# A convolution and a gated MLP in one kernel: how x is loaded and turned, how block 0 is convolved, and how far the second layer runs behind

## The chip, the cores and the metric

The kernel runs on one core of a Trainium2 chip. Its engines work side by side, each through its own queue in order: TensorE (PE in the profile; PEld are its weight loads), VectorE (DVE), ScalarE (ACT), GpSimd (POOL), and SyncE (SP), which here only issues DMAs and passes marks on. The metric is the device time of one execution in microseconds, the median over runs.

## The reference

x is 8 sequences of 4096 tokens with 192 columns, float32. Each of 8 heads (24 columns each) has 7 taps, passed through a softmax; the causal convolution sums a token and the six before it. Then a gated MLP with 1536 hidden columns follows:

```python
w = np.exp(weight - weight.max(-1, keepdims=True)); w = w / (w.sum(-1, keepdims=True) + 1e-9)
x_pad = np.concatenate([zeros(B, 6, D), x], axis=1)
out = np.einsum('hk,bskhg->bshg', w, windows_of_7(x_pad))     # per head h, tap k
g = out.reshape(B*S, D) @ w_gate                               # 192 -> 1536
val = out.reshape(B*S, D) @ w_val
return (g / (1 + np.exp(-g)) * val) @ w_out                    # 1536 -> 192
```

## The kernel before

**Tiles.** The 32768 tokens are 64 blocks of 512; two blocks make a pair (32 pairs). Hidden columns are 12 chunks of 128. So there are 768 chunks in all, and 24 per pair; "chunk c" below counts from the start of the run, or within a pair's 24 where it says so. The convolution works on columns in partitions and tokens along the row. A pair's 2 x 192 columns are three groups of 128 partitions: group 0 (A of the first block), group 1 (the last columns of one block with columns of the other), group 2.

**First layer.** `Block.first(j)` makes gate and val of chunk j: three matmuls of 64 rows each for gate (array rows 0 to 63) and three for val (rows 64 to 127), side by side in the array. Since a group's halves are needed on both halves of the array, each convolved group `xc` also has a copy `xs` with its halves swapped, made by two DMAs (`Group.swap`). PSUM holds 2 gate and 3 val tiles. `Block.gate(j)` lets ScalarE make silu (L318) and VectorE multiply h = silu x val (L320).

**Second layer.** `Block.second(n)` emits units. A block has 48: two halves of the tokens, in each two passes (the swap) over j = 0 to 11. Unit u of a half reads h of chunk j = u mod 12. A unit is two matmuls of 64 rows (`piece`, L325), one for each half of the array; the weights loaded are pieces of h. Here each chunk j of a block does four units of the block before: `first(j)` comes ahead of them, except where a half ends (j = 5 and 11); there the units come first, then ScalarE empties the accumulator (L363, an evacuation) and then `first(j)` follows. After the last unit of the first pass a mark is set: a no-op on SyncE that waits for it, and the first unit of the second pass waits for the mark.

**The convolution of later pairs.** `emit_cast` lets GpSimd issue a DMA that casts x to float16 in DRAM, `emit_turn` a transposing DMA from there. For each group ScalarE makes the product of tap 0 in PSUM (`start_d`, L249) and of two taps in SBUF (`act_tap`, L253), VectorE adds two taps to tap 0 (`dve_tap`, L260), GpSimd makes two products (L267), adds the parts (L273) and joins them (L277). An order written out by hand sets this: `at_chunk(c, f)` puts f behind chunk c's silu and h on every queue. For pair q the groups begin at chunk 24q-27, 24q-19 and 24q-11, their VectorE taps come 1 and 3 chunks later, ScalarE's 2 and 4, GpSimd's work 4, the swap 11.

**The opening.** x of pair 0 is loaded as it lies, cast by ScalarE and GpSimd, and turned by TensorE. The softmax is made on 8 partitions and spread by small matmuls. A0 and A1 are convolved by products as above; only group B goes through 14 matmuls with diagonal matrices (L390). Two swaps go through TensorE. The first weights come as float32 and are cast by ScalarE and GpSimd. All of this stands ahead of chunk 0, and VectorE's four taps of A1 (L260) stand ahead of its first h.

**The end.** When no first layer is left, the last block's 48 units follow, then copies and stores.

Of the kernel before, what the change touches and what calls it, by code (L numbers as in the profile page):

```python
# [12 lines left out]
PLAN = dict(  # L13
    start=(-27, -19, -11),
    first=(6, 10, 16),
    aD=0, aP=(2, 4), taps=(1, 3), pool=4, swap=11,
    cast=-54, turn=-40,
    nact=2, npool=2, gate=2, val=3,
)
# [3 lines left out]
def kernel(  # L23
# [9 lines left out]
    nc = tc.nc  # L33
# [30 lines left out]
    dpool = ctx.enter_context(tc.tile_pool(name="x16d", bufs=3, space=bass.MemoryType.DRAM))  # L64
# [3 lines left out]
    HIST = 16  # L68
    ROWS = HIST + TB
    drams, xts = {}, {}  # L70

    def emit_cast(q):
        t0 = q * 2 * TB - HIST
        d = dpool.tile([ROWS, 2 * D], fp16, tag="x16d", name="x16d")
        src = bass.AP(
            tensor=x_flat.tensor,
            offset=x_flat[t0 : t0 + 1, :].offset,
            ap=[[D, ROWS], [TB * D, 2], [1, D]],
        )
        nc.gpsimd.dma_start(out=d[:, :].rearrange("r (b c) -> r b c", b=2), in_=src)  # L80
        drams[q] = d

    def emit_turn(q):
        xt = xpool.tile([P, 3, ROWS], fp16, tag="xt", name="xt", bufs=3)
        nc.sync.dma_start(out=xt[:, :, :], in_=drams.pop(q)[:, :], transpose=True)
        xts[q] = xt

    def emit_blank(q):
        nc.scalar.copy(xts[q][:, 0, 0:HIST], zeros[:, 0:HIST])
        nc.scalar.copy(xts[q][0:DB, 1, 0:HIST], zeros[0:DB, 0:HIST])  # L90

    def sync_after(ins, earlier, why="one bank, two halves of the array"):
# [8 lines left out]
    taps = const_pool.tile([H, K], fp32, tag="taps", name="taps")  # L101
    nc.sync.dma_start(out=taps, in_=weight)
    x_sb = xpool.tile([P, 2 * SUBS, D], fp32, tag="x_sb", name="x_sb", bufs=1)
    halves = [
        nc.sync.dma_start(
            out=x_sb[:, b * SUBS : (b + 1) * SUBS, :],
            in_=x_flat[b * TB : (b + 1) * TB, :].rearrange("(s p) d -> p s d", p=P),
        )
        for b in range(2)
    ]  # L110

    C1 = 4 * P
    w = wpool.tile([P, 3, Dff], fp16, tag="w_sb", name="w_sb")
    w_st = wpool.tile([P, 3, C1], fp32, tag="w_st", name="w_st")
# [5 lines left out]
    for rows, src in w_halves:  # L120
        sync_after(
            nc.sync.dma_start(out=w_st[rows, :, :], in_=src[:, :, 0:C1]), halves[0], "x goes first"
        )

    def load_w(lo, hi, which):
        rows, src = w_halves[which]
        nc.gpsimd.dma_start(out=w[rows, :, lo:hi], in_=src[:, :, lo:hi])

    ident32 = const_pool.tile([P, P], fp32, tag="ident32", name="ident32")
    make_identity(nc, ident32)  # L130
    ident = const_pool.tile([P, P], fp16, tag="ident", name="ident")
    nc.vector.tensor_copy(ident, ident32)

    swapper = const_pool.tile([P, P], fp16, tag="swapper", name="swapper")
    nc.vector.tensor_copy(swapper[:, 0:DB], ident[:, DB:P])
    nc.vector.tensor_copy(swapper[:, DB:P], ident[:, 0:DB])
# [4 lines left out]

    opening = ctx.enter_context(ExitStack())
    pool0 = opening.enter_context(tc.tile_pool(name="xts0", bufs=1, space=bass.MemoryType.PSUM))


    zeros = const_pool.tile([P, TB], fp16, tag="zeros", name="zeros")
    nc.vector.memset(zeros, 0.0)
    early = {
        n: pool0.tile(shape, dt, tag=n, name=n)
        for n, shape, dt in (  # L150
            ("xt_act", [P, DB + TB], fp16),
            ("wn_ps", [P, 3, K], fp32),
            ("xtB", [P, DB + TB], fp16),
            ("xt", [P, DB + TB], fp16),
            ("sumB", [P, TB], fp32),
            ("swB", [P, TB], fp32),
            ("idle", [P, TB], fp32),
            ("xtC", [P, DB + TB], fp16),
        )
    }  # L160
    idle = early["idle"]

    def warm(n):
        for _ in range(n):
            nc.tensor.matmul(idle, ident, zeros, start=True, stop=True)  # L165


    own = const_pool.tile([H, 2 * D], fp32, tag="own", name="own")
    nc.gpsimd.memset(own, 1.0)
    for m in (own[:, 0:D], own[:, D:]):  # L170
        nc.gpsimd.affine_select(
            out=m, in_=m, pattern=[[1, D]],
            compare_op=ALU.is_ge, fill=0.0, base=0, channel_multiplier=-grp,
        )
        nc.gpsimd.affine_select(
            out=m, in_=m, pattern=[[-1, D]],
            compare_op=ALU.is_ge, fill=0.0, base=grp - 1, channel_multiplier=grp,
        )
    head = {n: const_pool.tile([H, 1], fp32, tag=n, name=n) for n in ("wmax", "wsum", "wrec")}
    soft = const_pool.tile([H, K], fp32, tag="soft", name="soft")  # L180
    warm(4)
    nc.vector.tensor_reduce(head["wmax"], taps, axis=AX.X, op=ALU.max, negate=True)  # L182
    nc.scalar.activation(soft, taps, AF.Exp, bias=head["wmax"])
    nc.scalar.activation(two, one, AF.Silu)
    nc.vector.tensor_reduce(head["wsum"], soft, axis=AX.X, op=ALU.add)
    nc.vector.tensor_scalar(head["wsum"], head["wsum"], scalar1=1e-9, scalar2=None, op0=ALU.add)
    nc.vector.reciprocal(head["wrec"], head["wsum"])
    nc.vector.tensor_scalar(soft, soft, scalar1=head["wrec"], scalar2=None, op0=ALU.mult)

    wn_ps = early["wn_ps"]  # L190
    wn = const_pool.tile([P, 3, K], fp32, tag="wn", name="wn")
    for g in range(3):
        nc.tensor.matmul(wn_ps[:, g, :], own[:, ts(g, P)], soft, start=True, stop=True)  # L193
    warm(2)
    nc.vector.tensor_copy(wn, wn_ps)

    x16 = xpool.tile([P, 1 + SUBS, 2, D], fp16, tag="x16", name="x16", bufs=1)
    nc.gpsimd.memset(x16[:, 0, 0, :], 0.0)
    nc.gpsimd.tensor_copy(x16[:, 1:, 0, 0:P], x_sb[:, 0:SUBS, 0:P])
    nc.scalar.copy(x16[:, 1:, 0, P:D], x_sb[:, 0:SUBS, P:D])  # L200
    nc.scalar.copy(x16[:, :, 1, 0:DB], x_sb[:, SUBS - 1 :, 0:DB])
    nc.gpsimd.tensor_copy(x16[:, :, 1, DB:D], x_sb[:, SUBS - 1 :, DB:D])
    for b in range(2):
        load_w(C1, 2 * C1, b)

# [8 lines left out]

    class Group:


        def __init__(self, p, g, pool=cpool):
            self.p, self.g, self.w, self.pool = p, g, wn[:, g, :], pool
            if p:  # L220
                self.xc_in = xts[p][:, g, HIST - pad :]
            self.parts = []

        def rows(self, s):
            return x16[:, s, :, :].rearrange("p b c -> p (b c)")[:, ts(self.g, P)]

        def turn(self, xt, reader=None):
            nc.tensor.transpose(xt[:, 0:DB], self.rows(0)[DB:P, :], ident[DB:P, DB:P])
            for s in range(SUBS):
                nc.tensor.transpose(xt[:, DB + s * P :][:, 0:P], self.rows(s + 1), ident)  # L230
            if reader == "act":
                self.xt_act = xt
            else:
                self.xt = xt

        def tap(self, k, psum=True, xt=None):
            v = (xt or self.xt)[:, DB - pad + k :][:, 0:TB] if psum else self.xc_in[:, k : k + TB]
            return v, self.w[:, k : k + 1]

        def copy(self):  # L240
            self.xc_in = self.pool.tile([P, pad + TB], fp16, tag="xcin", name="xcin")
            nc.scalar.copy(self.xc_in, self.xt[:, DB - pad :])

        def start_d(self, psum=True, xt=None):
            if self.p:
                self.aD = tpool.tile([P, TB], fp32, tag="run", name="run")
            else:
                self.aD = self.pool.tile([P, TB], fp32, tag="aD", name="aD")
            nc.scalar.mul(self.aD, *self.tap(0, psum, xt))  # L249

        def act_tap(self, k, psum=True, xt=None):
            self.parts.append(self.pool.tile([P, TB], fp32, tag=f"t{k}", name=f"t{k}"))
            nc.scalar.mul(self.parts[-1], *self.tap(k, psum, xt))  # L253

        def dve_tap(self, k, psum=False, last=False):
            v, s = self.tap(k, psum)
            run = self.aD
            if last:
                self.aD = self.pool.tile([P, TB], fp32, tag="aD", name="aD")
            nc.vector.scalar_tensor_tensor(  # L260
                out=self.aD, in0=v, scalar=s, in1=run, op0=ALU.mult, op1=ALU.add
            )

        def pool_tap(self, k):
            self.parts.append(self.pool.tile([P, TB], fp32, tag=f"t{k}", name=f"t{k}"))
            v, s = self.tap(k, False)
            nc.gpsimd.tensor_scalar(self.parts[-1], v, scalar1=s, scalar2=1.0, op0=ALU.mult, op1=ALU.mult)  # L267
            self.add()

        def add(self):  # L270
            if len(self.parts) > 1:
                t = self.parts.pop()
                nc.gpsimd.tensor_tensor(self.parts[0], self.parts[0], t, op=ALU.add)  # L273
# [112 lines left out]
    for i, d in enumerate(diag):  # L386
        if i:
            A1.turn(early["xtC"])
# [157 lines left out]
```

## Time and profile before

| what | us |
|---|---|
| three runs | 780.5, 780.53, 781.44 (median 780.53) |
| the profiled execution | 780.98 |
| its span, first to last instruction | 779.2 |
| first matmul of chunk 0 (L313) | 15.47 |
| first h (L320) | 19.26 |
| chunk 24's third matmul step (L314) | 44.35 |
| last h of all | 771.81 to 772.50 |
| last copies of the output | 775.84 |

Mean durations of single operations, from the groups of instructions: h 0.685, silu 0.593, a VectorE tap 0.742 to 0.749, a ScalarE product 0.713, a GpSimd product 0.828, a GpSimd sum 1.269, an evacuation 0.479. Operations of one queue overlap a little, so the distance from one start to the next is shorter than the duration; the timeline shows it.

How to read the lines shown below. A line of the timeline has start, duration, engine, line of the code, operation, output and inputs, and in brackets how long the engine was idle before it and what ended that. A row of the stretch table has the stretch, its length, then busy time (with the number of instructions) of PE, PEld, DVE, ACT and POOL, the granted TensorE clock (1.00 is full), the share of time in which the 16 DMA engines were busy, and GB/s.

### The profile page before, as it was taken

What the parts mean: (1) busy time and instruction counts of PE and PEld (TensorE: products, weight loads), DVE (VectorE), ACT (ScalarE), POOL (GpSimd) and SP (SyncE); (2) the same over time, 40 slices, a digit from 0 to 9 for tenths busy, and PEclk for the clock granted to TensorE, in tenths of its full rate; (3) what the DMA queues carried; (4) which work ended last, traced back from release to release, by engine and by line L of the source; (5) the groups of instructions that cost most, each with busy time, mean ns of one, the idle gap of its engine ahead of it and who ended that gap; (6) DMA issues with size and microseconds to landing.
All of it is one profiled execution on the core that took longest, in us unless ns stands there. A gap on an engine that the chain in (4) does not pass through costs nothing.

```text
span 779.2 us, 27410 instructions
## 1 busy us (share of the span) xinstructions
PE 767.4 (98%) x10800; PEld 587.8 (75%) x10800; DVE 632.8 (81%) x980; ACT 661.0 (85%) x1207; POOL 647.7 (83%) x612
## 2 busy tenths in 40 slices
PE   7899999999999999999999999999999999999998
PEld 3567777777777777777777777777777777777776
DVE  6778888888888888888888888888888888888874
ACT  6788888888888888888888888888888888888874
POOL 6799988888888988888988888988888988888820
PEclk9999999999999999999999999999999999999999
DMA  8643553543444454434443435443435443624111
GB/s 154 105 96 67 95 81 89 96 96 68 94 79 93 94 78 86 95 74 98 92 89 77 94 73 99 91 90 77 95 68 102 91 88 81 94 69 103 46 46 53
DMA packets 137186, 67.36 MB, mean 86 GB/s; under 512 B 90080, under 2 KB 136672, under 8 KB 137056
## 3 DMA queue, kind: packets, MB, share of 16 engines
q1 hardware_dynamic: 101440, 51.65, 26.2%
q0 software_dynamic: 35616, 13.95, 16.7%
q8 instruction: 84, 1.38, 0.7%
q14 instruction: 46, 0.38, 0.2%
HBM read 29.47 MB, written 37.74 MB: 86 GB/s over the span
## 4 chain that ended last, share of the span: by engine, by line
PE 97%; ACT 1%; POOL 1%; DMA 0%; DVE 0%; issue 0%; SPq 0%; POOLq 0%; DVEq 0%; ACTq 0%
PE val L314 49%; PE acc L325 34%; PE gate L313 11%; PE sumB L390 1%; ACT silu L318 1%; DMA xs<-xc 0%; PE idle L165 0%; POOL t L273 0%; ACT t L253 0%; DVE h L320 0%; PE wn_ps L193 0%; POOL xc L277 0%; PE gate L325 0%; PE val L325 0%; ACT xc L398 0%
## 5 line engine op out<-in xcount | busy, mean ns | idle before, releaser
L320 DVE TENSOR_TENSOR h<-silu,val 128x512 f16<-128x512 f16 x768 | 512.5, 685 | 133.6 <-ACT silu L318 97.7
L318 ACT ACTIVATE silu<-gate 128x512 f16<-128x512 f32 x768 | 449.3, 593 | 83.2 <-PE gate L313 80.0
L325 PE MATMUL acc<-wo_sb,h 64*128 64x192 f16 x6096 | 474.7, 243 | 0.2 <-DVE h L320 0.2
L325 PEld LDWEIGHTS <-h 64*128 64x128 f16 x6144 | 402.2, 94 | 65.9 <-issue 2.6
L313 PE MATMUL gate<-xs,w_sb 64*128 64x512 f16 x1152 | 428.9, 377 | 1.3 <-ACT silu L318 1.3
L313 PE MATMUL gate<-xc,w_sb 64*128 64x512 f16 x1152 | 428.4, 377 | 1.0 <-ACT silu L318 0.9
L273 POOL TENSOR_TENSOR t<-t,t 128x512 f32<-128x512 f32 x281 | 356.6, 1269 | 85.4 <-ACT t L253 51.6
L314 PE MATMUL val<-xc,w_sb 64*128 64x512 f16 x1152 | 424.0, 377 | 1.1 <-DVE h L320 1.0
L314 PE MATMUL val<-xs,w_sb 64*128 64x512 f16 x1152 | 373.2, 377 | 1.7 <-DMA xs<-xc 1.7
L314 PEld LDWEIGHTS <-w_sb 64*128 64x128 f16 x2304 | 209.4, 94 | 106.9 <-issue 6.0
L313 PEld LDWEIGHTS <-w_sb 64*128 64x128 f16 x2304 | 209.8, 94 | 6.2 <-issue 3.2
L267 POOL TENSOR_SCALAR t<-xt,wn 128x512 f32<-128x512 f16 x186 | 139.0, 828 | 2.2 <-DMA xt<-x16d 2.2
L253 ACT ACTIVATE t<-xt,wn 128x512 f32<-128x512 f16 x186 | 132.6, 713 | 0.0
L277 POOL TENSOR_TENSOR xc<-t,aD 128x512 f16<-128x512 f32 x94 | 119.0, 1266 | 8.0 <-DVE aD L260 0.7
L363 ACT COPY o<-acc 128x384 f32<-128x384 f32 x126 | 60.3, 479 | 20.6 <-PE acc L325 9.1
L260 DVE SCALAR_TENSOR_TENSOR run<-xt,wn,run 128x512 f32<-128x512 f16 x93 | 69.7, 749 | 0.0
L260 DVE SCALAR_TENSOR_TENSOR aD<-xt,wn,run 128x512 f32<-128x512 f16 x93 | 69.0, 742 | 0.0
L249 ACT ACTIVATE run<-xt,wn 128x512 f32<-128x512 f16 x93 | 63.8, 686 | 1.1 <-DVE aD L260 1.1
L80 POOL DMA_DIRECT2D x16d<-in_x_dram x31 | 39.1, 1261 | 0.0
L165 PE MATMUL idle<-zeros,ident 128*128 128x512 f16 x6 | 2.9, 620 | 2.6 <-DVE wmax L182 2.6
L390 PE MATMUL sumB<-xcin,diag 128*128 128x512 f16 x14 | 5.1, 525 | 0.0
L260 DVE SCALAR_TENSOR_TENSOR aD<-xcin,wn,aD 128x512 f32<-128x512 f16 x4 | 3.9, 971 | 0.1
(73 smaller groups left out, 51.3 us busy)
## 6 DMA issues: line engine op xcount, KB each, us to landing
out_dram<-o SPq DMA_DIRECT2D x128, 192.0 KB, 2.2
x16d<-in_x_dram POOLq DMA_DIRECT2D x31, 396.0 KB, 6.1
xs<-xc SPq DMA_DIRECT2D x188, 64.0 KB, 2.8
x_sb<-in_x_dram SPq DMA_DIRECT2D x2, 384.0 KB, 3.6
wo_sb<-in_moe_w_out_dram POOLq DMA_DIRECT2D x1, 576.0 KB, 8.3
xt<-x16d SPq DMA_TRANSPOSE x31, 4.0
w_st<-in_moe_w_gate_dram SPq DMA_DIRECT2D x1, 384.0 KB, 4.4
w_st<-in_moe_w_val_dram SPq DMA_DIRECT2D x1, 384.0 KB, 5.3
```

Source lines behind the costliest of these rows:

```text
L249: nc.scalar.mul(self.aD, *self.tap(0, psum, xt))
L253: nc.scalar.mul(self.parts[-1], *self.tap(k, psum, xt))
L260: nc.vector.scalar_tensor_tensor(out=self.aD, in0=v, scalar=s, in1=run, op0=ALU.mult, op1=ALU.add)
L267: nc.gpsimd.tensor_scalar(self.parts[-1], v, scalar1=s, scalar2=1.0, op0=ALU.mult, op1=ALU.mult)
L273: nc.gpsimd.tensor_tensor(self.parts[0], self.parts[0], t, op=ALU.add)
L277: (eng or nc.gpsimd).tensor_tensor(xc, self.parts[0], self.aD, op=ALU.add)
L313: nc.tensor.matmul(g, w[0:DB, ca, f], a[0:DB, :], start=(i == 0), stop=(i == 2))
L314: nc.tensor.matmul(v, w[DB:P, cb, f], b[DB:P, :], start=(i == 0), stop=(i == 2))
L318: nc.scalar.activation(s, self.g.pop(j), AF.Silu)
L320: nc.vector.tensor_tensor(h, s, self.v.pop(j), op=ALU.mult)
L325: ins = nc.tensor.matmul(acc, self.h[j][r, ts(s, P)], wo_r[r, j, :], start=first and j == 0, stop=not first and j == NCH - 1, skip_group_c ...
L363: nc.scalar.copy(self.o[:, 2 * half : 2 * half + 2, :], self.acc[:, :, 0:D])
```

## The change

**Loads and turns of later pairs.** No cast and no transposing DMA. For pair q, `emit_load` issues eight DMAs on SyncE's queue, two at each of chunks 24q-41, -40, -38 and -37. They bring x as float32 in squares of 32 tokens by 32 columns; each piece is 128 bytes. Tile sqA holds 128 columns of both blocks (1056 wide, with 32 tokens of history), sqB the last 64 columns of the first block and below them those of the second (544 wide). `emit_turn` lets VectorE transpose all squares of a group in one instruction (544, 544 and 512 wide).

**Groups.** They begin two chunks earlier: 24q-29, -21 and -13. Transposes stand two chunks ahead of that. Counted within a pair's 24 chunks: transposes in 17, 1 and 9; tap 0 in 19, 3, 11; ScalarE's products in 21, 23; 5, 7; 13, 15; VectorE's taps in 20, 22; 4; 12, 14. Group 1 has one VectorE tap and three GpSimd products; the others have two and two. Pair 1 has a plan of its own (`opening`): group 0 and 1 have three GpSimd products each.

**Second layer.** `lead=8`: chunks 8 to 11 of block 0 do two units each of block 0 itself. After that, each block's chunks 10 and 11 do its own units 0 to 7, and chunks 0 to 9 the remaining 40 of the block before. The accumulator is emptied in chunks 3 and 9. The end has 40 units left, ordered so that the ones which read h of the last two chunks come after the others of the first pass.

**Opening.** x comes in three DMAs (256, 256 and 512 tokens). The taps are loaded to all 128 partitions, and the softmax is made there by VectorE and ScalarE without matmuls. The first four chunks' weights are cast by GpSimd's DMA. Block 0's A is convolved with diagonal matrices in two parts (`hi`, `lo`) and its last columns, high and low part stacked, with one (`dgC`). The diagonal matrices are built from `twin`, two identities side by side, so the results need no swap. The last columns of block 1 are turned and convolved on TensorE between chunks 0 and 5 (`lateC`); A1 stays with taps: two on ScalarE, five on VectorE.

The core of the diff:

```diff
 PLAN = dict(
-    start=(-27, -19, -11),
-    first=(6, 10, 16),
-    aD=0, aP=(2, 4), taps=(1, 3), pool=4, swap=11,
-    cast=-54, turn=-40,
-    nact=2, npool=2, gate=2, val=3,
+    start=(-29, -21, -13), turn=-2,
+    acts=(2, 4), dves=(1, 3), pool=4, swap=11, swap2=(16, 14, 12), npool=(2, 3, 2),
+    load=(-41, -40, -38, -37),
+    opening=(
+        (3, 5, (8,), (7, 9), 4, 10, 14),
+        (9, 11, (12, 14), (13,), 11, 15, 22),
+        (14, 16, (18, 20), (17, 18), 20, 20, 28),
+    ),
+    gate=2, val=3, lead=8,
 )
...
+    def emit_load(q, part):
+        if part == 0:
+            squares[q, "A"] = xpool.tile([P, HIST + 2 * TB], fp32, tag="sqA", name="sqA")
+            squares[q, "B"] = xpool.tile([P, HIST + TB], fp32, tag="sqB", name="sqB")
+        for k in range(2):
+            quad = 2 * (part % 2) + k
...
+            nc.sync.dma_start(
+                out=tile_[quad * SQ : (quad + 1) * SQ, :].rearrange("p (n c) -> p n c", c=SQ),
+                in_=x_flat[row : row + n * SQ, c : c + SQ].rearrange("(n p) c -> p n c", p=SQ),
+            )
+
+    def emit_turn(q, g):
+        name, lo, hi = (("A", 0, HIST + TB), ("B", 0, HIST + TB), ("A", HIST + TB, HIST + 2 * TB))[g]
...
+        nc.vector.transpose(out=xts[q, name][:, lo:hi], in_=squares[q, name][:, lo:hi])
...
+    def conv_a(d, first):
+        for k in range(K):
+            for r, bank in ((slice(0, DB), "sum0"), (slice(DB, P), "sum1")):
+                nc.tensor.matmul(
+                    early[bank], d[r, k, :], xcA[r, k : k + TB],
+                    start=first and k == 0, stop=not first and k == K - 1,
+                )
...
+    def conv_c(bank, xc):
+        for k in range(K):
+            nc.tensor.matmul(
+                bank, dg["C"][:, k, :], xc[:, k : k + TB], start=k == 0, stop=k == K - 1
+            )
...
+    conv_a(dg["hi"], True)
+    turn(early["xtA1"], colA, SUBS, hist=True)
+    conv_a(dg["lo"], False)
+    conv_c(early["sum2"], xcC)
...
+    for n in range(2 * n_pairs):
+        block = Block(n)
+        for j in range(NCH):
+            src, units = before if j < NCH - lead // 4 else block, 4
+            if n == 0:
+                src, units = block, lead // 4 if j >= NCH - 4 else 0
+            los, his = src.second(units)
+            half = src.done // (2 * NCH) - 1 if units and src.done % (2 * NCH) == 0 else None
...
+            elif half is None:
+                block.first(j)
+            for lo, hi in zip(los, his):
+                lo()
+                hi()
+            if half is not None:
+                src.evacuate(half)
+                block.first(j)
+            block.gate(j)
...
+    run(0, 1, range(lead, NCH - 2), True)
+    run(2, 3, range(NCH - 2), True)
+    for j in range(NCH - 2, NCH):
+        run(0, 1, (j,), True)
+        run(2, 3, (j,), True)
+    run(1, 0, range(NCH), False)
...
+    run(3, 2, range(NCH), False)
```

## The prediction

> **What bounds the kernel now.** I read the page first (engine rows, then the chain that ended last), then the stretch table, then single stages in the timeline and the chain.
>
> ```profile
> span 779.2 us, 27410 instructions
> PE 767.4 (98%) x10800; PEld 587.8 (75%) x10800; DVE 632.8 (81%) x980; ACT 661.0 (85%) x1207; POOL 647.7 (83%) x612
> ...
> PE 97%; ACT 1%; POOL 1%; DMA 0%; DVE 0%; issue 0%; SPq 0%; POOLq 0%; DVEq 0%; ACTq 0%
> ```
>
> TensorE (PE) is busy 98% and is 97% of the chain. The stretch table (span, then busy time of PE, PEld, DVE, ACT, POOL, granted clock, DMA share, GB/s) says where it isn't:
>
> ```profile
> 16.00:19.90 3.90, 2.25 (x17) 0.71 (x14) 3.79 (x6) 2.96 (x6) 1.73 (x2) 1.00 1.38 189
> 19.90:23.30 3.40, 3.31 (x16) 1.36 (x17) 2.24 (x5) 1.19 (x2) 2.07 (x2) 0.50 1.39 194
> ...
> 44.35:770.00 725.65, 725.65 (x10395) 564.56 (x10396) 598.23 (x921) 627.13 (x1147) 615.72 (x571) 1.00 0.42 84
> ```
>
> From 44.35 to 770 TensorE never stops: the chain's pieces repeat every 5.865 us per six chunks (764.05 less 758.19), 0.9775 a chunk. Only work that stops TensorE there, or what lies before 44.35, can move the time. Before 44.35 the chain waits for VectorE's taps of the second block, then for GpSimd's last sum of pair 1 and its swap:
>
> ```profile
> 15.35 3.99 DVE L260 SCALAR_TENSOR_TENSOR aD<-xcin,wn,aD 128x512 f32<-128x512 f16 x4
> 19.26 1.87 DVE L320 TENSOR_TENSOR h<-silu,val 128x512 f16<-128x512 f16 x3
> ```
> ```profile
> 38.72 1.28 POOL xc L277
> 40.02 0.46 SPq L283
> ...
> 40.53 3.78 DMA xs<-xc
> ```
>
> One steady chunk, which the forecast hangs on (start, duration):
>
> ```profile
> 762.18 0.38 PE L313 MATMUL gate<-xs,w_sb 64*128 64x512 f16 x1
> ...
> 762.83 0.52 PE L325 MATMUL acc<-wo_sb,h 64*128 64x192 f16 x6
> 763.03 0.60 ACT L318 ACTIVATE silu<-gate 128x512 f16<-128x512 f32 x1 [0.38 <-PE gate L313]
> ...
> 763.16 0.38 PE L313 MATMUL gate<-xs,w_sb 64*128 64x512 f16 x1
> ...
> 763.66 0.69 DVE L320 TENSOR_TENSOR h<-silu,val 128x512 f16<-128x512 f16 x1 [0.29 <-ACT silu L318]
> ```
>
> Call a chunk's start T (here 762.18). Units of the second layer start at T+0.65, one each 0.08; silu starts at T+0.85, h at T+1.48 and ends at T+2.17. TensorE feels it 0.04 later: in the last chunk h ends at 772.50 and its reader starts here:
>
> ```profile
> 772.55 0.26 PE L325 MATMUL acc<-wo_sb,h 64*128 64x192 f16 x2 [0.21 <-DVE h L320]
> ```
>
> **The change, part by part.**
>
> *Second layer ten chunks behind.* With lead=8, the first chunk of each block does units 8 to 11 of the block before; unit 11 reads h of the chunk just before. In the built order its weight load carries a wait for VectorE, in each of 63 blocks. Let T be the start of that previous, twelfth chunk. The load would issue 0.20 after the units start, at T+0.9775+0.65+0.20 = T+1.83; h arrives at T+2.21. So TensorE stops at least 0.38 us per block. Behind the load stand all later chunks; nothing on TensorE fills the gap.
>
> VectorE can be late on top. In the rows one h follows another after 0.60 (708.39, then 708.99), and a tap holds the queue 0.66 (708.99 to 709.65):
>
> ```profile
> 707.15 0.69 ACT L249 ACTIVATE run<-xt,wn 128x512 f32<-128x512 f16 x1
> 707.77 1.12 ACT L318 ACTIVATE silu<-gate 128x512 f16<-128x512 f32 x2
> ```
> ```profile
> 708.39 0.69 DVE L320 TENSOR_TENSOR h<-silu,val 128x512 f16<-128x512 f16 x1 [0.41 <-ACT silu L318]
> 708.99 0.75 DVE L260 SCALAR_TENSOR_TENSOR run<-xt,wn,run 128x512 f32<-128x512 f16 x1
> 709.65 1.28 DVE L320 TENSOR_TENSOR h<-silu,val 128x512 f16<-128x512 f16 x2
> ```
>
> Here a ScalarE product behind an evacuation's late silu made the next silu late, and a VectorE tap behind that h made the following one start at T+2.21 (709.65; its T is 707.44). The new plan puts this pattern on chunks 21 to 23 of each pair: evacuation and ScalarE tap in 21, VectorE tap in 22. So h of chunk 23 is 0.73 late (2.21 against 1.48): the stop is 0.38+0.73 = 1.11. On chunks 9 to 11: evacuation in 9 (its h starts at T+1.80, as 707.29 does after 705.49), the transpose behind it. I price its 512 columns like a tap, 0.66, the nearest VectorE row of that size; bounds are half of that and twice. h of 10 then starts at 1.80+0.60+0.66 = 3.06, h of 11 at 3.66, which counted from chunk 11 is 1.71 instead of 1.48: 0.23 late, the stop is 0.61. At half price it is the bare 0.38; at twice, 1.27.
>
> Pairs 1 to 30 have the 0.61, pairs 2 to 30 the 1.11 at their end, and the last pair two bare stops: 30x0.61 + 29x1.11 + 2x0.38 = 51.3 us. (The ends of pair 0 and pair 1 lie in the opening, below.)
>
> *Other steady work, per pair of 23.46 us before (24x0.9775), now some 25.1.* VectorE: 24 h at 0.60, 5 taps (one fewer) at 0.66 and 3 transposes at about 0.66 make 19.7. ScalarE: nothing but places moved. GpSimd: the cast's 1.26 goes; one product (0.68 apart, 1.36 for two) and one sum (1.3) come: its 20.5 in the stretch 300 to 323.46 becomes 21.2. That its products now read f32 I price at nothing; the f16 row has 0.83, the cast of f32 0.61. All fit, so they cost nothing but the lateness above. DMA: the cast and the transposing DMA go; 4x1056 + 4x544 = 6,400 packets of 128 B come. At the hardware queue's mean of 32 ns (26.2% of 16x779.2 us over 101,440) they use 12.8 us of 16 engines, half the pair. Loads are issued 10 or more chunks before their transpose, so they hide. SyncE's queue: eight more issues. These are ahead of the mark that lets unit 12 start; at 0.5 each (a swap's 0.46 to 0.60) four, a store, four more end about when the mark's matmul does. That costs nothing up to about 0.65; a later rival takes the rest.
>
> *Opening.* Three ends decide it. (1) x comes in quarters (first about 3.6, from 384 KB landing 3.3 after issue), the softmax needs no matmul, the first diagonals are there about 5.2; convolution of A from about 6: 7 paired steps at 0.43 (L390 cold), 0.7 of transposes (an xt group), 14 more steps of which some five are cold and the others 0.21: about 13.0, with bounds 12.4 and 13.9 for when the clock rises. Three PSUM copies and a product on ScalarE, and the first chunk is done at 14.3. (2) VectorE finishes A1's taps first (A1 turned about 10.4, then 0.7+4x0.78 as L260's four took 3.11: 14.2), so h begins at 14.9 instead of 19.26. (3) Pair 1 then bounds it: first transpose after the fourth h, 18.2 to 18.9; GpSimd's first group waits for its taps and ends at 26.7, the second takes 3x0.68 + 5x1.3 = 8.5, to 35.2; the swap stands in SyncE's queue behind chunk 21's store, issue 37.1, 3.9 to land: 41.0. Chunk 24's third step starts there instead of 44.35: -3.4 us. Bounds -1 (GpSimd a group later by the two DMA copies of weights in front) and -6 (swap in the median 2.8, store not in the way). Late h's at chunks 11 and 23 are inside this (the latter about 40.7).
>
> *Tail.* 40 units instead of 48: 8x0.082 = 0.65, and the 0.21 wait goes: -0.9.
>
> Sum on the profiled execution: 779.2 - 3.4 - 0.9 + 51.3 = 826.2 span; plus 1.8 outside the span (780.98 less 779.2), less 0.45 by which that execution lies above the median 780.53: **828 us**. Its own bounds: opening ±2.5, transpose half (-7) or a third dearer (+7), refilling TensorE after each stop (0 to 0.1, +6): 815 to 842.
>
> **Rivals.**
> (a) *Bare stops.* VectorE's lateness doesn't add, since each stop gives it time. For: DVE is idle 19% of the span. Against: the lateness arises within three chunks, after the gap. 62x0.38 = 23.6: 800.
> (b) *Dear transposes.* At twice a tap (1.32) the odd stop is 1.27: 30x0.66 = 20 more, 848. For: f32, and this engine's tap with both inputs in SBUF took 0.97 against 0.75 (L260, aD<-xcin and aD<-xt), so something is shared. Against: a transpose has one input. The Trainium skill ("SBUF — State Buffer", Who interferes with whom) says a VectorE copy that runs in a two-port mode and a GpSimd instruction lock each other out for a whole instruction; no transpose is in this trace to show whether it is one of these.
> (c) *Clock.* TensorE idled 42% of 16 to 19.9 and then got 0.50; idle 34% of 27 to 31, it kept 1.00 (2.64 busy of 4.00). A stop of 1.11 in 3.4 us is 33%. From above that share each pair end would run 3.4 us at half clock, 1.7 lost: 29x1.7 = 49, 877. The Trainium skill ("TensorE: Matmul & The Clock Gate", Part 1) puts the fall after an idle window of about 3.4 us; by that these stops never cost clock. The row at 16 to 19.9 fell with less idle time than that.
> (d) *SyncE late.* From 0.65 per load issue the mark of unit 11 comes late; at 0.75 (the longest plain issue, w_st) about 0.65 a pair, 848; at 1.31 (a transposing issue) 5 a pair, 980. For: 1,056 pieces an issue. Against: issues of 64 to 512 pieces take 0.38 to 0.75 without order.
> (e) *Faster.* If TensorE doesn't stop for h, only opening and tail remain: 776. It needs h within 1.40 us of the last gate matmul's start (T+0.43 to T+1.83); the steady rows have 1.78.
>
> **How the numbers follow.** Forecast 0.60; (a) 0.13; (b) 0.08; (c) 0.06; (d) 0.05; (e) 0.06, something unseen within 0.2% 0.02. 797 to 851 holds the forecast, (a), (b) and the mild half of (d), some 0.83. The clock's 877 and 776 stay out. Faster by over 0.2% (what a measurement of this kernel can tell) is (e) with 0.06, the same 0.02, slower 0.92. The likeliest's own range is 815 to 842.
>
> **What would show it.** Right: a wait of TensorE's weight loads for h some 60 times, about 0.6 and 1.1 in turn; TensorE under 94% busy; chunk 24 near 41; transposes near 0.7; no long wait for SyncE. Wrong: TensorE without gaps after 45; equal stops near 0.4 (a); transposes above 1.2 (b); stages at half clock (c); weight loads waiting for SyncE's nop (d).

## The result, and the profile after

The changed kernel takes 874.43 us (median of four runs, 871.73 to 876.9) against 780.51 before: a ratio of 1.1201, with a 95% interval of 1.116 to 1.1241. The forecast was 828, its range 797 to 851. The direction was right, and the loss is nearly twice the one forecast. The profiled execution of the changed kernel is the one of 871.73, with a span of 870.0. The four runs differ as their mean granted clocks do: 871.73 at 0.998, 872.76 at 0.997, 876.1 and 876.9 at 0.994.

The page of the changed kernel, its engine rows, granted clock and chain:

```profile
span 870.0 us, 27810 instructions
...
PE 787.9 (91%) x10821; PEld 484.1 (56%) x10821; DVE 668.2 (77%) x1046; ACT 662.2 (76%) x1206; POOL 668.7 (77%) x639
...
PEclk9999999999999999999999999999999999999999
...
PE 70%; SPq 10%; DVE 7%; issue 6%; ACT 4%; DMA 2%; POOL 1%; ACTq 0%; DVEq 0%
```

TensorE's share of the span falls from 98% to 91%, with a granted clock of nine tenths or more in every slice; a slice is 21.7 us long, so a short fall of the clock doesn't show here. Its share of the chain falls from 97% to 70%. What is new in the chain is SPq, SyncE's issuing of DMAs, with 10%, more than VectorE's 7%.

The view of who waited for whom (total us, times, longest us), with the lines that concern TensorE's second layer (L417) and the history columns' blanking (L103):

```profile
PEld L417 <- DVE h L412: 50.2, 63, 1.1
PEld L417 <- SPq L312: 40.4, 30, 2.7
...
PE acc L417 <- SPq L312: 25.7, 28, 2.2
...
ACT xtA L103 <- DVE xtA L100: 10.3, 7, 1.5
ACT xtB L103 <- DVE xtB L100: 9.9, 7, 1.4
```

The wait for h is there 63 times and 50.2 us long, as forecast (51.3). Beside it stand two things that the forecast had left at nothing: 30 waits for the mark on SyncE (L312), and ScalarE's waits for VectorE at the seven sequence starts.

To see where each loss lies I took the times from one evacuation copy (L455) to the next out of the trace. Before the change every such half block takes 5.865 us. What it takes more is the loss there. An interval is "even" where it holds the end of a pair (chunk 24 and its multiples), "odd" where it holds the end of a pair's first block (chunk 12 of the pair), and "mid" otherwise. The last column compares the evacuation of chunk 27, or 29 with `lead=0`, to the same place before the change (49.33 at chunk 29, so 47.37 at chunk 27). Names of experiments are explained below.

| kernel | median us | even, sum of 30 | odd, sum of 31 | mid, sum of 62 | opening to chunk 27 or 29 |
|---|---|---|---|---|---|
| before | 780.51 | 0.0 | 0.0 | 0.0 | 0 |
| changed | 874.43 | 39.7 | 47.2 | 5.1 | -0.4 |
| lead=0 | 795.18 | 5.2 | 0.2 | 11.6 | -2.6 |
| loads spread | 841.95 | 39.7 | 17.8 | 3.7 | -0.2 |
| blank by VectorE | 863.99 | 33.4 | 53.1 | 0.4 | -1.2 |
| tap in chunk 21 | 860.55 | 25.9 | 51.7 | 3.8 | -0.8 |
| lead=8, three mends | 817.58 | 19.4 | 17.7 | 0.2 | -0.2 |
| old kernel, lead=8 | 830.03 | 33.4 | 12.9 | 0.0 | +1.9 |
| lead=0, four mends | 783.31 | -0.2 | 1.7 | 2.5 | -2.0 |
| lead=0, loads behind its marks | 779.95 | -0.2 | 0.0 | 1.7 | -2.9 |

In the changed kernel the even loss is 1.14 to 1.15 at most pairs, and 2.05 at the seven sequence starts. The odd loss is different in each pair, from 0.36 to 3.23.

**An even boundary**, in the timeline of the changed kernel (start, duration, engine, line, operation; in brackets the idle time before and what ended it):

```profile
707.10 1.07 ACT L410 ACTIVATE silu<-gate 128x512 f16<-128x512 f32 x2
...
707.72 0.69 DVE L412 TENSOR_TENSOR h<-silu,val 128x512 f16<-128x512 f16 x1 [0.40 <-ACT silu L410]
...
708.33 0.74 DVE L352 SCALAR_TENSOR_TENSOR aD<-xtA,wn,run 128x512 f32<-128x512 f32 x1
...
708.98 1.28 DVE L412 TENSOR_TENSOR h<-silu,val 128x512 f16<-128x512 f16 x2
709.72 0.10 PEld L417 LDWEIGHTS <-h 64*128 64x128 f16 x2 [1.13 <-DVE h L412]
```

From its wait of 0.40 on VectorE runs h, tap, h, h without a gap, as the forecast had it from the old kernel's rows, and TensorE's load of unit 11 stands still for 1.13 us.

**An odd boundary**, half a pair later, with SyncE's queue beside TensorE's second layer (x4 means four issues in a row; L318 and L319 are a swap, L89 the loads, L447 the store, L455 the evacuation of chunk 9):

```profile
716.07 0.46 SPq L318 DMA_DIRECT2D xs<-xc  x1
...
716.59 0.59 SPq L319 DMA_DIRECT2D xs<-xc  x1
...
717.27 2.84 SPq L89 DMA_DIRECT2D sqA<-in_x_dram  x4
...
718.17 0.48 ACT L455 COPY o<-acc 128x384 f32<-128x384 f32 x1
...
720.20 0.52 SPq L447 DMA_DIRECT2D out_dram<-o  x1
...
720.76 2.14 SPq L89 DMA_DIRECT2D sqB<-in_x_dram  x4
...
721.97 0.10 PEld L417 LDWEIGHTS <-h 64*128 64x128 f16 x2 [0.50 <-DVE h L412]
...
723.09 0.28 PEld L417 LDWEIGHTS <-h 64*128 64x128 f16 x8 [0.70 <-SPq L312]
```

SyncE's own waits from 714 to 724 are one line:

```profile
SPq L312 <- PE acc L417: 2.7, 1, 2.7
```

So until 715.95 SyncE waits at the mark of chunk 6, which stands in its queue ahead of everything here. Then it issues a swap, four loads, the store (the evacuation it needs had ended at 718.65, and it goes out at 720.20), four more loads, and only then comes to the mark that lets unit 12 start. TensorE pays twice: 0.50 for h, then 0.70 for the mark. In the 28 pairs from pair 2 to pair 29, the loss of the interval is the end of the eighth load, counted from the evacuation of chunk 9, less 3.82 us (correlation 0.995). Every pair keeps to this within 0.01 but pair 17, which loses 0.35 more; the clock, below, explains it.

**A sequence start**, every fourth pair:

```profile
728.51 0.74 DVE L100 STREAM_TRANSPOSE xtA<-sqA 128x544 f32<-128x544 f32 x1
...
729.28 0.22 ACT L103 CAST xtA<-zeros 128x32 f32<-128x32 f16 x1 [1.48 <-DVE xtA L100]
729.40 1.08 ACT L410 ACTIVATE silu<-gate 128x512 f16<-128x512 f32 x2
...
730.03 1.28 DVE L412 TENSOR_TENSOR h<-silu,val 128x512 f16<-128x512 f16 x2 [0.78 <-ACT silu L410]
730.05 0.37 PE L405 MATMUL gate<-xc,w_sb 64*128 64x512 f16 x1 [0.59 <-ACT silu L410]
```

ScalarE's copy of zeros waits 1.48 us for VectorE's transpose of the same chunk. The silu behind it comes late, the gate's bank comes free late, and TensorE stands still for 0.59 us.

### The profile page after: what moved, and what is told of

Same layout as the page of the kernel before. It is cut to its first block, busy times and chain, and to the rows that moved or that the text cites. A ratio compares the mean times of both kernels' runs of the same rounds, so it can differ in the third digit from the quotient of the medians.

```text
span 870.0 us, 27810 instructions
## 1 busy us (share of the span) xinstructions
PE 787.9 (91%) x10821; PEld 484.1 (56%) x10821; DVE 668.2 (77%) x1046; ACT 662.2 (76%) x1206; POOL 668.7 (77%) x639
## 4 chain that ended last, share of the span: by engine, by line
PE 70%; SPq 10%; DVE 7%; issue 6%; ACT 4%; DMA 2%; POOL 1%; ACTq 0%; DVEq 0%
PE gate L405 44%; PE acc L417 24%; SPq L89 8%; DVE h L412 4%; ACT silu L410 3%; PE val L406 1%; DVE aD L352 1%; SPq L447 1%; DMA x_sb<-in_x_dram 1%; DVE xtA L100 1%; DVE xtB L100 1%; ACT run L342 1%; DMA sqB<-in_x_dram 0%; SPq L319 0%; ACT t L335 0%
## 5 line engine op out<-in xcount | busy, mean ns | idle before, releaser
L417 PE MATMUL acc<-wo_sb,h 64*128 64x192 f16 x6096 | 369.5, 243 | 64.0 <-DVE h L412 38.0
L417 PEld LDWEIGHTS <-h 64*128 64x128 f16 x6144 | 275.2, 94 | 233.7 <-DVE h L412 50.2
L405 PE MATMUL gate<-xs,w_sb 64*128 64x512 f16 x1128 | 365.4, 377 | 0.0
L357 POOL TENSOR_SCALAR t<-xtB,wn 128x512 f32<-128x512 f32 x93 | 63.9, 696 | 34.8 <-DVE xtB L100 25.0
L335 ACT ACTIVATE t<-xtA,wn 128x512 f32<-128x512 f32 x123 | 88.1, 716 | 0.0
L357 POOL TENSOR_SCALAR t<-xtA,wn 128x512 f32<-128x512 f32 x125 | 85.3, 695 | 3.5 <-DVE xtA L100 3.2
L455 ACT COPY o<-acc 128x384 f32<-128x384 f32 x126 | 60.2, 478 | 4.4 <-PE acc L417 0.4
L352 DVE SCALAR_TENSOR_TENSOR run<-xtA,wn,run 128x512 f32<-128x512 f32 x62 | 46.5, 750 | 0.0
L352 DVE SCALAR_TENSOR_TENSOR aD<-xtA,wn,run 128x512 f32<-128x512 f32 x62 | 46.0, 742 | 0.0
L100 DVE STREAM_TRANSPOSE xtA<-sqA 128x544 f32<-128x544 f32 (+1 forms) x62 | 44.7, 722 | 0.0
L335 ACT ACTIVATE t<-xtB,wn 128x512 f32<-128x512 f32 x62 | 44.2, 713 | 0.0
```

The source lines that it names most:

```text
L100: nc.vector.transpose(out=xts[q, name][:, lo:hi], in_=squares[q, name][:, lo:hi])
L335: mul(parts[-1], *self.tap(k))
L352: nc.vector.scalar_tensor_tensor(out=self.aD, in0=v, scalar=s, in1=run, op0=ALU.mult, op1=ALU.add)
L357: self.product(k, lambda t, v, s: nc.gpsimd.tensor_scalar(t, v, scalar1=s, scalar2=1.0, op0=ALU.mult, op1=ALU.mult), self.parts)
L405: nc.tensor.matmul(g, w[0:DB, ca, f], a[0:DB, :], start=(i == 0), stop=(i == 2))
L417: ins = nc.tensor.matmul(acc, self.h[j][r, ts(s, P)], wo_r[r, j, :], start=first and j == 0, stop=not first and j == NCH - 1, skip_group_c ...
```

## The experiments

Each run was compared with the kernel before on the same chip, whose median lay between 780.16 and 780.45. Where an edit adds a line ahead of the helpers, their line numbers are one higher than in the changed kernel.

**lead=0.** The second layer runs twelve chunks behind again; all else is the change.

```diff
-    gate=2, val=3, lead=8,
+    gate=2, val=3, lead=0,
...
-    acc = before.acc
+    acc = apool.tile([P, 2, 512], fp32, tag="acc", name="acc")
```

> The changed kernel with the second layer twelve chunks behind again (lead=0), everything else as changed. My theory: nearly all of the loss at the blocks' starts comes from unit 11's need of the h of the chunk just before and from the mark on SyncE that follows it; both get two chunks (1.96 us) of slack. The intervals from evacuation to evacuation show 29 even stops of 1.14, 30 odd ones of 1.55 in the mean; without them 874.4 - 33 - 46 + 0.8 (longer tail) = about 796, with the 9.6 us of the blank copies still in it: 790 to 801, and no weight load waits for h more than five times. Rival 1, only the wait for h goes and SyncE stays late behind its loads: -51, about 824. Rival 2, VectorE's queue or the DMA traffic bounds the loop whatever the order: over 850.

Measured 795.18 (794.94 to 795.73), ratio 1.0185 [1.0171, 1.02]. The page and the waits:

```profile
span 793.4 us, 27810 instructions
...
PE 771.4 (97%) x10821; PEld 515.1 (65%) x10821; DVE 663.6 (84%) x1046; ACT 658.3 (83%) x1206; POOL 669.5 (84%) x639
```
```profile
PEld L417 <- SPq L312: 5.0, 6, 1.7
```

The wait for h is gone from the list, and the odd loss falls from 47.2 to 0.2. So both losses at the boundaries hang on unit 11's place. The traffic, the transposes and the f32 taps are still there, and they cost next to nothing in the steady loop. What stays is the sequence starts, 1.01 and 0.74 at each of them, and a few late marks (5.0 us of waits in six times).

**Loads spread.** The same issues at other places of SyncE's queue.

```diff
-        for part, c in enumerate(PLAN["load"]):
+        for part, c in enumerate(PLAN["load"] if q < 4 else (-60, -54, -48, -42)):
```

> Only the places of the load issues of pairs 4 and later change: two issues right behind each of four marks (chunks -60, -54, -48, -42 of the pair) instead of eight issues ahead of one mark; as many bytes and packets. My theory: the mark at the odd block's start stands in SyncE's queue behind eight issues of 0.5 to 0.7 us, and that is what makes the odd stop 1.55 instead of the 0.61 forecast; 28 times 0.94 = 26 us go: 848 (842 to 854), and the waits of the weight loads for SyncE's mark (30 times, 40 us) drop below 5 us. Rival: the odd stop is VectorE's, from the transpose behind the evacuation's late h: no change (872 to 877).

Measured 841.95 (840.02 to 842.8), ratio 1.078 [1.0761, 1.0798]: 32.5 us less than the change, more than expected. The same boundary in its timeline:

```profile
690.52 1.15 SPq L89 DMA_DIRECT2D sqB<-in_x_dram  x2
...
691.97 0.40 SPq L447 DMA_DIRECT2D out_dram<-o  x1
...
695.26 0.10 PEld L417 LDWEIGHTS <-h 64*128 64x128 f16 x2 [0.50 <-DVE h L412]
...
695.74 0.92 SPq L89 DMA_DIRECT2D sqA<-in_x_dram  x2
...
695.79 0.48 PEld L417 LDWEIGHTS <-h 64*128 64x128 f16 x8
```

The wait for h is the same 0.50. The mark's wait is gone, and the next two loads go out behind the mark. The odd loss is now 0.51 to 0.53 in 29 of 31 pairs. So nearly all of the scatter of 0.36 to 3.23 came from the issues ahead of the mark, and not from VectorE and not from the traffic, which is unchanged.

**Blank by VectorE.**

```diff
-            nc.scalar.copy(xts[q, name][rows, 0:HIST], zeros[rows, 0:HIST])
+            nc.vector.memset(xts[q, name][rows, 0:HIST], 0.0)
```

> The blanking of the 32 history columns at each sequence's start by VectorE behind its own transpose, instead of by ScalarE, which waits for VectorE. My theory: at the seven sequence starts ScalarE's copies wait up to 1.5 us for the transposes, silu and then the gate's bank come late, 1.38 us more each than at other pairs: -9.6 us, 865 (862 to 868), and the three waits around the blank copies vanish from the list. Rival: the sequence start's loss is in GpSimd's or SyncE's work, or VectorE loses as much by the two small writes: no change (872 to 877).

Measured 863.99 (861.53 to 865.83), ratio 1.1063 [1.1036, 1.1091]: 10.4 us less. ScalarE's two waits for the transposes are no longer in the list. GpSimd's wait for ScalarE's copy only changes its partner: it now waits for VectorE's blanking, 9.4 us in seven times. The even loss is the same at sequence starts as elsewhere, and the mid loss falls from 5.1 to 0.4. The odd loss happens to be 53.1 in this profile, which is SyncE's scatter, with two stretches of 3.41 us at half clock in it (from 269.39 and from 481.01).

**Tap in chunk 21.**

```diff
-                [c + o for o in PLAN["dves"][: 4 - PLAN["npool"][g]]],
+                [c + o for o in ((1, 2) if g == 0 else PLAN["dves"][: 4 - PLAN["npool"][g]])],
```

> Only the second VectorE tap of each pair's first group moves, from chunk 22 to chunk 21 (after the h of chunk 21 instead of after that of chunk 22). My theory: this tap, behind a late h, makes the h of chunk 23 0.73 us later; without it the even stop falls from 1.14 to the bare 0.38: -22 us, 852 (846 to 860). Rival 1: the evacuation on ScalarE and its late silu alone make the stop, the tap is hidden: no change (872 to 877). Rival 2: the tap delays the h of chunk 22 instead, which nothing waits for, but the delay is handed on in full to 23: also no change.

Measured 860.55 (860.28 to 863.15), ratio 1.1029 [1.101, 1.1048]: 13.9 us less, two thirds of what was expected. The even boundary in its timeline:

```profile
698.42 0.74 DVE L352 SCALAR_TENSOR_TENSOR aD<-xtA,wn,run 128x512 f32<-128x512 f32 x1
...
699.08 2.10 DVE L412 TENSOR_TENSOR h<-silu,val 128x512 f16<-128x512 f16 x3
...
700.41 0.10 PEld L417 LDWEIGHTS <-h 64*128 64x128 f16 x2 [0.50 <-DVE h L412]
```

The load's wait falls from 1.13 to 0.50, the interval's loss from 1.14 to 0.65. So the tap was worth 0.49, not 0.73. Without it three h still run back to back behind the tap's new place. That leaves 0.27 above the bare 0.38, and which of ScalarE's products makes it was not taken apart. Two stretches of 3.41 us at half clock (from 267.71 and from 479.33) are part of this profile's odd loss.

**Old kernel with lead=8.** Nothing but the order of the second layer is taken from the change.

```diff
+    lead = 8
...
-                los, his = before.second(4) if before is not None else ([], [])
+            src, units = before if j < NCH - lead // 4 else block, 4
+            if n == 0:
+                src, units = block, lead // 4 if j >= NCH - 4 else 0
+            los, his = src.second(units)
...
-        for j in range(NCH):
+        for j in range(lead if (lo, hi) == (0, 1) else 0, NCH):
```

> The kernel before with the change's second layer ten chunks behind and nothing else of the change: cast, transposing DMA, taps and opening as before. My theory: the stop at each block's start comes with lead=8 by itself. In this plan the evacuations fall on chunks 9 and 21 of a pair, a ScalarE product on 21 and a VectorE tap on 22, so the even stop should be the forecast's 1.11 (31 of them), and the odd one, with no VectorE tap behind chunk 9, the bare 0.38 (32): 780.5 + 34 + 12 - 0.9 = 826 (818 to 832). SyncE has no eight issues in a row, so no wait for its mark. Rival 1: only bare stops, 63 x 0.38 - 0.9: 804. Rival 2: the stops need the new transposes on VectorE or the f32 taps; the old kernel with lead=8 stays within 785.

Measured 830.03 (828.36 to 831.69), ratio 1.0641 [1.0621, 1.0661]. In its view of the waits (L325 is the second layer there, L320 makes h):

```profile
PEld L325 <- DVE h L320: 51.0, 65, 1.9
```

The even loss is 1.08, and 1.32 at sequence starts, the odd one 0.42, and nothing waits for SyncE. So `lead=8` alone costs some 50 us, in a kernel without VectorE's transposes and without square loads. That pair 0's own boundaries lie in the opening shows as well: chunk 27 comes 1.9 us later than before.

**Pair 1's loads held back**, on top of `lead=0`.

```diff
...
-        nc.sync.dma_start(
+        x_last = nc.sync.dma_start(
...
+        sync_after(nc.sync.nop(), x_last, "x goes first")
         for part in range(4):
             emit_load(1, part)
```

> The changed kernel with lead=0 (795.2 measured), and pair 1's square loads held back until the last quarter of x has landed. My theory: these loads share the DMA engines with x's last quarter (8.4 us to land) and the taps (4.2 us), and that cost the opening most of the 3.4 us forecast: with x alone the last quarter lands some 3 us earlier, block 1's convolution begins earlier, and chunk 29 ends 2 to 3 us earlier: 792.5 (791.5 to 794). Rival 1: the opening is bound by the taps' landing and the softmax, the diagonal matmuls and GpSimd's sums, which x's last quarter doesn't move: 795 (794.5 to 796). Rival 2: pair 1's loads then land after 19 us, its first transpose waits and the opening loses: 796 to 799.

Measured 796.46 (796.02 to 796.87), ratio 1.0206 [1.0192, 1.0221]: 1.3 us slower, as rival 2 had it; 0.6 of it is there by chunk 29. SyncE's queue in its timeline:

```profile
9.11 2.37 SPq L89 DMA_DIRECT2D sqA<-in_x_dram  x4
11.52 8.17 SPq L89 DMA_DIRECT2D sqB<-in_x_dram  x4
19.80 1.44 SPq L319 DMA_DIRECT2D xs<-xA  x1
```

x's last DMA (512 tokens) lands 7.33 us after its issue. Without the edit it took 6.07 in the run with lead=0 and 8.43 in the changed kernel, and with it 8.10 in the run with all four mends below. So no gain from holding the loads back shows in it. The four sqB issues now take 8.17 us (5.82 with lead=0 alone), and A1's swap stands behind them until 19.80 (17.56 without the edit). My theory of the opening fell.

**All four mends, lead=0 and lead=4.** Both have the blanking, the spread and the held-back loads of the runs above, whose edits are left out here; they differ in `lead`.

```diff
...
-    gate=2, val=3, lead=8,
+    gate=2, val=3, lead=0,
...
-    acc = before.acc
+    acc = apool.tile([P, 2, 512], fp32, tag="acc", name="acc")
```
```diff
...
-    gate=2, val=3, lead=8,
+    gate=2, val=3, lead=4,
...
```

> All four mends together: second layer twelve chunks behind (lead=0), loads of pairs 4 and later spread behind four marks, blanking by VectorE, pair 1's loads behind x. My theory: from 795.2 go 12.3 us at the seven sequence starts (intervals 6.88 and 6.61 against 5.87 in the run with lead=0), 2 to 3 us of single late marks and 0.05 us stops, and 2 us or so in the opening: 778.5 (776 to 781), level with the kernel before or up to 0.6% faster. Rival: the terms aren't independent, with ScalarE's wait gone VectorE, 84% busy, is late at the same places: 785 to 790.

> As the run with all four mends, with the second layer eleven chunks behind (lead=4) instead of twelve. My theory: h then has 0.98 us more than with lead=8, against a stop of 1.11 to 1.14 at the even and 0.52 at the odd boundary: 0.15 us left at some 30 boundaries, 4.5 us, less 0.4 of tail: 4 us slower than the run with lead=0, 783. Rival: lateness doesn't add once TensorE runs on, so no wait is left and the tail's 0.4 makes it faster than lead=0, 778.

Measured 783.31 (782.82 to 783.71), ratio 1.0038 [1.0025, 1.0052], with lead=0, and 807.61 (807.51 to 807.72), ratio 1.0349 [1.0335, 1.0364], with lead=4. With lead=0 it lies between my figure and the rival's. The 12.3 us at the sequence starts are gone in full (the even loss is -0.2), so those terms are independent; but the held-back loads lose in the opening instead of gaining, the mark of chunk 38 still comes 2.0 late and costs 1.7, and smaller stops make 2.5. With lead=4 both figures on record, 783 and 778, were missed. The waits are:

```profile
PEld L418 <- SPq L313: 25.7, 40, 4.0
...
PEld L418 <- DVE h L413: 4.5, 29, 0.2
```

The wait for h came out as expected to the tenth, 4.5 us in 29 times. What I had not thought of is that the marks move with lead: with lead=4 they fall on chunks 1, 7, 13 and 19 of a pair, each one chunk behind two loads. The late ones are those of chunk 7 (28 times) and chunk 1 (9 times), where a swap and two sqB loads lie ahead of the mark. Behind issues of the usual length the mark of chunk 7 is 0.2 late; in nearly all waits above 0.5 one of the four issues took 0.9 to 2.0. One wait of 4.0 lies in pair 1, where the loads of pair 3 have their old places. How the 24.3 us between the two runs divide was not taken apart beyond that.

**Loads right behind the marks of lead=0**, pair 1's loads where the change has them, blanking by VectorE.

```diff
-    gate=2, val=3, lead=8,
+    gate=2, val=3, lead=0,
...
-            nc.scalar.copy(xts[q, name][rows, 0:HIST], zeros[rows, 0:HIST])
+            nc.vector.memset(xts[q, name][rows, 0:HIST], 0.0)
...
-        for part, c in enumerate(PLAN["load"]):
+        for part, c in enumerate(PLAN["load"] if q < 3 else (-58 + (q == 3), -52, -46, -40)):
...
```

> lead=0, blanking by VectorE, pair 1's loads where the change has them, and from pair 3 on two load issues right behind each of four marks (chunks -58, -52, -46, -40, two later than in the run with four mends, since with lead=0 the marks fall two chunks later). My theory: holding pair 1's loads back cost 1.3 us, so 783.3 becomes 782.0; the single late mark at chunk 35 (1.68) and some 1.5 us of later ones (0.70, 0.26, 0.22 and so on) come from loads issued up to two chunks ahead of a mark and go: 779 (777.5 to 780.5), level with the kernel before. Rival: the late marks come from swaps and stores, not from the loads: 782.

Measured 779.95 (779.08 to 780.35, eleven runs), ratio 0.9992 [0.9983, 1.0001]: level with the kernel before. Its page:

```profile
span 777.7 us, 27839 instructions
...
PE 768.2 (99%) x10821; PEld 547.8 (70%) x10821; DVE 663.4 (85%) x1060; ACT 658.4 (85%) x1192; POOL 667.3 (86%) x639
...
PE 96%; DMA 1%; SPq 1%; ACT 1%; DVE 1%; POOL 0%; issue 0%; DVEq 0%; ACTq 0%
```

TensorE is the bound again. The opening has gained 2.9 us up to chunk 29; 1.5 us of small stops in the loop give half of it back.

**lead=8 with three mends**: loads spread, blanking by VectorE, tap in chunk 21.

```diff
-        for part, c in enumerate(PLAN["load"]):
+        for part, c in enumerate(PLAN["load"] if q < 4 else (-60, -54, -48, -42)):
...
-            nc.scalar.copy(xts[q, name][rows, 0:HIST], zeros[rows, 0:HIST])
+            nc.vector.memset(xts[q, name][rows, 0:HIST], 0.0)
...
-                [c + o for o in PLAN["dves"][: 4 - PLAN["npool"][g]]],
+                [c + o for o in ((1, 2) if g == 0 else PLAN["dves"][: 4 - PLAN["npool"][g]])],
```

> Still ten chunks behind (lead=8), with the loads behind the marks, the blanking by VectorE and the group's second tap in chunk 21. My theory: the three terms lie at different places (odd boundaries, sequence starts, even boundaries) and add: 874.4 - 32.4 - 10.4 - 13.8 = 818 (815 to 821), which leaves the wait for h of chunk 11's kind, 0.52 and 0.65 in turn. Rival: VectorE's lateness is handed from one place to the next, so that part of each gain is lost: 825 to 835.

Measured 817.58 (816.0 to 818.51), ratio 1.0473 [1.0456, 1.0489]. The three terms add to within half a microsecond. What is left, 0.52 and 0.65 in turn, is the price of unit 11 reading the h of the chunk just before.

## Why the prediction was right in direction and wrong in size

The forecast's span was 826.2, the profiled one 870.0, 43.8 us more. Term by term, from the intervals of the changed kernel:

| term | forecast | measured | difference |
|---|---|---|---|
| stops for h | 51.3 | 29 x 1.14 + 0.36 even, 16.0 odd = 49.4 | -1.9 |
| SyncE's marks | 0 | 47.2 - 16.0 odd, less 0.35 of clock = 30.8 | +30.8 |
| half clock, once | 0 | 0.35 odd, 1.34 mid = 1.7 | +1.7 |
| sequence starts | 0 | 39.7 - 33.4 even, 5.1 - 1.34 mid = 10.1 | +10.1 |
| opening | -3.4 | -0.4 | +3.0 |
| tail | -0.9 | -0.8 | +0.1 |

(The 16.0 is the odd sum of the run with spread loads, 17.8, less the 1.8 that one late mark, that of chunk 36, adds in it.)

**Right: the stops for h.** The bare stop is 0.36 (0.38 forecast), seen in the last pair. The even one is 1.14 (1.11), the odd one 0.52 (0.61). The old kernel with lead=8 alone loses the same way, and lead=0 removes all of it. The forecast's 0.73 on top of the bare stop was the price of a pattern, a ScalarE product behind an evacuation and then a VectorE tap; the run that moved the tap shows that the tap makes 0.49 of it.

**Right: the transposes.** They take 0.722 in the mean from sqA and 0.739 from sqB, and the next h starts 0.66 after a transpose does, the value taken. The rival of dear transposes fell. The page named there ("SBUF — State Buffer", Who interferes with whom, in the Trainium skill) says that a VectorE copy in a two-port mode and a GpSimd instruction lock each other out; here nothing of the kind shows, since no transpose takes over 0.74 and GpSimd's sums keep 1.268 (1.269 before) beside 93 transposes.

**Wrong: SyncE's queue.** This is the step that failed: "at 0.5 each (a swap's 0.46 to 0.60) four, a store, four more end about when the mark's matmul does. That costs nothing up to about 0.65". Two things were wrong in it. The count began with the first load, but SyncE is held by the mark of chunk 6 and goes on only 2.1 us before the evacuation of chunk 9, and then issues group 0's swap first, 1.2 us with its gaps. And the issues are dearer than priced: in the same 28 pairs the eight loads have a mean of 0.63 and a sum of 5.0 instead of 4.0, since single ones last far longer. From mark to mark there is room for 6.4 us of issues (2.1 and 3.8, and 0.5 in which TensorE stands for h anyway); the best pair needs 6.7, the median 7.5. At 0.5 a load the same queue would take about 6.1, and without the swap the median pair 6.3, so by this estimate it took both errors to make the mark of a usual pair late. The mechanism stood there as rival (d) with a chance of 0.05. Its threshold of 0.65 an issue was wrong for the same reason: at a mean of 0.63 it already costs 1.1 us a pair.

**Wrong: "ScalarE: nothing but places moved."** The blanking moved from a place where it never waited (the fourteen copies of the old kernel show no idle time ahead of them) to one right behind a transpose of the same chunk, where ScalarE waits 1.4 to 1.5 us, twice per sequence start. Blanking by VectorE gave 10.4 us back.

**Off in size: the opening.** Chunk 24's third step was forecast at 41.0 and starts at 43.93. The end of its chain:

```profile
40.43 0.38 ACT o L455
40.82 0.41 SPq L447
41.32 0.47 SPq L318
41.84 2.04 DMA xs<-xc
43.93 0.26 PE val L406
```

The mechanism is the one forecast, a swap behind chunk 21's store in SyncE's queue. It issues at 41.32 instead of 37.1, and lands in 2.04 instead of 3.9. Late is chunk 21 itself. The first diagonal matrices were put at 5.2, but VectorE waits for the taps until 4.96 and begins the diagonals at 7.41, behind the softmax; the first h comes at 17.12 instead of 14.9. Pair 0's own two boundaries add some 2 us, which the forecast held to be "inside this": with lead=0 the opening gains 2.6 to 2.9 us. That the square loads of pair 1 cost the rest is not borne out, since holding them back made it slower.

**Clock.** The rival put half a clock behind every pair end, 49 us. That fell, and that its 877 lies near the measured 874.43 is chance. But the thing itself came once, behind the dearest odd boundary of all, pair 17's, where the weight load waited 0.5 for h and 2.7 for the mark. In the stretch table:

```profile
480.86:484.27 3.41, 1.32 (x23) 0.97 (x25) 1.23 (x2) 1.34 (x3) 2.49 (x2) 1.00 0.75 150
484.27:487.68 3.41, 3.41 (x28) 1.75 (x26) 1.98 (x3) 2.15 (x4) 0.00 (x0) 0.50 0.31 89
```

The clock is the third figure from the end. Half of it for 3.41 us loses 1.7 us of work. That is the 0.35 by which pair 17's odd interval loses more than its queue makes it, and the 1.34 of the mid interval behind, which holds no late mark. A stop of 1.14 never did this in the changed kernel, so the forecast's limit of a third idle was too low. The changes of the clock lie whole multiples of 3.41 us apart, and I divided all twelve traces into such stretches. Behind each in which TensorE was busy for less than 1.53 us the clock fell to 0.50; behind none with more than 1.83 did it; between the two it went either way. The page named there (the Trainium skill, "TensorE: Matmul & The Clock Gate", Part 1) puts the fall after an idle window of about 3.4 us. The traces agree with the length and not with the idleness: TensorE was busy for 1.32 us of the 3.41 here.

## What to carry to other kernels

When a step adds entries to a queue, write out the whole queue between two waits of that queue, with what stood there already, and compare it with the time between the waits; a price per entry says nothing by itself. A no-op that passes a mark on in a queue of DMA issues is as late as the issues ahead of it, so put new issues right behind a mark, and put them there again whenever the marks move. When two halves of a loop are brought closer, ask for each reader whether it now reads what was made one step before, and take the time from the producer's slowest case.

## What the runs showed of the hardware

- Issues of one shape differ widely: the 124 sqA issues of the changed kernel took 0.347 to 4.896 us, with a median of 0.594; in the run with spread loads 0.311 to 4.952, median 0.556. What makes single ones long was not settled. Where they lie behind a mark, they cost nothing.
- The granted clock fell to 0.50 for 3.41 us behind a stretch of 3.41 us in which TensorE had been busy for 1.32 (changed kernel), 1.39 and 1.49 (blank by VectorE), 0.90 and 1.52 (tap in chunk 21). A mean clock of 0.998 over the run hides one such fall.
- GpSimd's product of f32 takes 0.695 us, the one of f16 before the change took 0.828.
- A transpose of 32 by 32 squares, 128x544 in f32, takes VectorE 0.74 us, about as long as a tap.
